# Weighting of v and the next tile's scores in one block, with the scores in the transposes' PSUM banks

## The chip, the cores and the metric

The kernel runs on one core of a Trainium2 chip. The metric is the device time of one execution in microseconds; the time given for a kernel is the median of its timed runs. Inside the core TensorE multiplies matrices into PSUM (eight banks), VectorE (DVE in the profile), ScalarE (ACT) and GpSimd (POOL) work on vectors, and the DMA queues move data between the chip's memory and the on-chip buffers. The engines run beside each other and wait for one another through semaphores.

## The reference

Attention within chunks of 64 tokens, for 8 batches, 8 heads, 576 tokens and 64 values per head. Its output, with the heads laid side by side (512 values per token), goes through a Fourier mix over tokens and values, a normalisation and a two-layer network with a hidden size of 2048:

```python
scores = scale * np.matmul(q_c, k_c.transpose(0, 1, 2, 4, 3))     # q_c, k_c, v_c: (8, 8, 9, 64, 64)
scores = scores - np.max(scores, axis=-1, keepdims=True)
attn = np.exp(scores)
attn = attn / (np.sum(attn, axis=-1, keepdims=True) + 1e-09)
x = np.matmul(attn, v_c)                                          # then laid out as (8, 576, 512)
...
X = np.fft.fft(x, axis=1)
X = np.fft.fft(X, axis=2)
u = x + np.real(X).astype(np.float32)
un = (u - mu) / np.sqrt(var + 1e-06)                              # over the 512 values
ch = np.maximum(un @ w_ch1, 0.0) @ w_ch2                          # w_ch1: 512x2048, w_ch2: 2048x512
return u + ch
```

All is in 32-bit floats; q, k, v and the weights arrive as 64-bit floats.

## The kernel before

**Tiles.** A tile is two chunks of 64 tokens with all heads: 128 rows by 512 values. A batch has nine chunks, so four tiles, and the ninth chunks of two batches make one tile more, which belongs to the even one: batches 0, 2, 4, 6 have five tiles, the odd ones four. For each tile n there are four steps of attention, called T, S, P and V here:

```python
    def att_T(n):                      # T: q and k of a tile, transposed
        if n >= first[2]:              # from the third batch on by VectorE, in stream transposes
            for src, dst, nm in ((qs, qT, "qT"), (ks, kT, "kT")):
                ...
                nc.vector.transpose(out=to.rearrange("p j c (r t) -> p j t c r", t=4), in_=a)
                if low:
                    nc.gpsimd.tensor_copy(t[:, :, :, 0:1], t[:, :, :, CH:CH + 1])
            if n + 1 < NT:
                load(n + 1)
            return
        ...                            # before that by TensorE (turn), copied out of PSUM by ScalarE

    def att_S(n):                      # S: 16 products of 64x64
        a, b = qT.pop(n), kT.pop(n)
        sc = ps_a.tile([128, 2, 512], FP32, tag="att", name="sc")
        ...
    def softmax(n):                    # maximum and difference on VectorE, exponential on ScalarE
        sc = scs.pop(n)
        ...
        nc.vector.tensor_reduce(out=mx, in_=s4, axis=AX.X, op=ALU.max)
        nc.vector.tensor_tensor(out=ex..., in0=s4, in1=mx..., op=ALU.subtract)
        nc.scalar.activation(out=ex, in_=ex, func=ACTF.Exp, scale=scale)

    def att_P(n):                      # P: the weights, transposed by TensorE, copied out by ScalarE
        ex = es.pop(n)
        pt = turn(lambda j: ex[:, j].rearrange("p e k -> p (e k)"))
        t = one_p.tile([128, NJ, 128], FP32, tag="pT", name="pT")
        nc.scalar.copy(t, pt)

    def att_V(n):                      # V: 16 products of 64x65, then sums and division on VectorE
        ...
            xp = ps_a.tile([128, 2, 512], FP32, tag="att", name="xp")
        ...
```

A 32-bit matmul is two passes of TensorE in the profile: the 16 matmuls of S or V count as x32 there.

**PSUM.** Two buffers of one bank serve all transposes (`turn`, four of 128x128 each) and the Fourier products; one buffer of two banks serves scores and weighted v in turn; four of one bank serve the network:

```python
    ps_t = ctx.enter_context(tc.tile_pool(name="ps_t", bufs=2, space=bass.MemoryType.PSUM))
    ps_a = ctx.enter_context(tc.tile_pool(name="ps_a", bufs=1, space=bass.MemoryType.PSUM))
    ps_f = ctx.enter_context(tc.tile_pool(name="ps_f", bufs=4, space=bass.MemoryType.PSUM))
```

**The side work of a batch.** The attention and the Fourier mix of batch b run in small steps (each `yield` ends one) between the steps of the network of an earlier group of four tiles:

```python
        for n in range(lo, hi + 1):
            att_S(n)
            softmax(n)
            yield
            if n + 1 < NT and (b > 0 or n < hi):
                att_T(n + 1)
            yield
            if n > lo:
                att_V(n - 1)
                ...
                yield ready(n - 1)
            att_P(n)
            yield
        att_V(hi)
```

**The network.** Nine groups of four tiles; the first groups use plain products, the later ones seven products in place of eight on halves (`up_halves` from group 2, `down_halves` from group 1). In `up_halves`, for each of four pairs r = 0, 1 of hidden blocks, products o = 0 to 6 are made, two blocks each, and read as follows (line numbers of the profile in the comments; L974 is the matmul):

```python
                    dst = (pas, pas, pbs, pbs, pas, pbs, pbs)[o][r][:, (0, 1, 0, 1, 0, 0, 1)[o]]
                    ...
                    if o == 0:
                        nc.scalar.copy(a, dst)                                            # L979
                    elif o == 1:
                        nc.vector.tensor_tensor(out=b, in0=dst, in1=a, op=ALU.add)        # L981
                    elif o == 2:
                        nc.vector.tensor_tensor(out=a, in0=dst, in1=b, op=ALU.add)        # L983
                    elif o == 3:
                        nc.vector.tensor_tensor(out=h1[:, HF + m, hi], in0=dst, in1=a, op=ALU.add)
                        ...
                if o in (1, 3, 5, 6):
                    yield h1
```

`pas[r]` and `pbs[r]` are one bank each. A step of side work follows each `yield`. `down_halves` (matmul L1021) has the same seven products and yields after each block; among them stand `normed` (the normalised tile `un` of the next group) and, one block later, `turned` (its transposes by `turn`, copied to `unT` by ScalarE or VectorE). In group 0's `down_plain` they stand so:

```python
            for j in range(G):
                due = KF - (G - j + 1)
                if m == due - 1:
                    normed(g + 1, j)
                if m == due:
                    turned(g + 1, j)
```

**The start.** Batch 0's attention (`attention_early`) and Fourier mix (`fourier_early`) run ahead of the network. The weights are made from 64-bit to 32-bit floats in 32 pieces by `round_next`: five VectorE operations and three ScalarE operations a call, each call finishing the piece of the one before. Two calls stand at the end of `attention_early`, one behind `fourier_early`, the others between the network's steps, ahead of the relus that ScalarE makes of the first products.

Of the kernel before, what the change touches and what calls it, by code (L numbers as in the profile page):

```python
# [8 lines left out]
FP32 = mybir.dt.float32  # L9
# [7 lines left out]
def kernel(  # L17
# [38 lines left out]
    NM = 2  # L56
    NT = 2 * 2 * NM + 1
# [15 lines left out]
    two_p = ctx.enter_context(tc.tile_pool(name="two", bufs=2))  # L73
    three_p = ctx.enter_context(tc.tile_pool(name="three", bufs=3))
    sm_p = ctx.enter_context(tc.tile_pool(name="sm", bufs=4))
    ps_t = ctx.enter_context(tc.tile_pool(name="ps_t", bufs=2, space=bass.MemoryType.PSUM))
    ps_a = ctx.enter_context(tc.tile_pool(name="ps_a", bufs=1, space=bass.MemoryType.PSUM))
    ps_f = ctx.enter_context(tc.tile_pool(name="ps_f", bufs=4, space=bass.MemoryType.PSUM))
    dram = ctx.enter_context(tc.tile_pool(name="dram", bufs=1, space=bass.MemoryType.DRAM))
# [35 lines left out]
    tiles, first = [], []  # L115
# [8 lines left out]
    NT = len(tiles)  # L124
# [159 lines left out]
    def round_weight(i):  # L284
# [15 lines left out]
        if 0 < i <= len(pieces):  # L300
# [8 lines left out]
                free.append(r)  # L309
            load_weight(max(raws, default=i - 1) + 1)  # L310

    def turn(src):

        pt = ps_t.tile([128, 4, 128], FP32, tag="pt", name="pt")
        for j in range(4):
            nc.tensor.transpose(pt[:, j, :], src(j), ident)  # L316
        return pt
# [39 lines left out]

    def att_S(n):
        a, b = qT.pop(n), kT.pop(n)
        sc = ps_a.tile([128, 2, 512], FP32, tag="att", name="sc")  # L360
        for j in range(NJ):
            for e in range(2):
                for c in range(2):
                    r0, t0 = e * D, c * CH
                    nc.tensor.matmul(
                        out=sc[t0:t0 + CH, e, j * CH:(j + 1) * CH],
                        lhsT=a[r0:r0 + D, 2 * j + c, 0:CH],
                        rhs=b[r0:r0 + D, 2 * j + c, 0:CH],
                        start=True,
                        stop=True,  # L370
                    )
        scs[n] = sc
# [16 lines left out]
    def att_P(n):  # L389
# [4 lines that stand above are left out]
        pT[n] = t  # L394
# [111 lines left out]
    def attention_early():  # L506

        lo, hi = first[0], first[1] - 1

        def ready(n):  # L510
            if n == at[LO, 0, 1]:
                shift_early(0)
            if n == at[HI, 0, 1]:
                fold(0, 1)
            if n == at[HI, 0, 0]:
                fold(0, 0)
            if n + 3 > hi:
                load_v(n + 3)

        att_T(lo)  # L520
        att_S(lo)
        for n in range(lo, hi + 1):
            if n < hi:
# [4 lines that stand above are left out]
                ready(n - 1)  # L528
            if n < hi:
                att_S(n + 1)  # L530
            if n in (lo, hi):
                keep_warm(1)
            att_P(n)
        shift_early(1)
        fold(0, NM)
        keep_warm(1)
        att_V(hi)
        ready(hi)
        keep_warm(3)
        turn_tables()  # L540
        round_next()
        round_next()

    def attention(b):

        lo, hi = first[b], first[b + 1] - 1

        def ready(n):

            if n == at[LO, b, NM - 1]:  # L550
                shift(b)
            for i in range(NM):
                if n == at[HI, b, i]:
                    fold(b, i)
            if n == at[HI, b, 0]:
                fold(b, NM)
            return kind(n) == HI

        if b < 2:
            att_T(lo)  # L560
            yield
        for n in range(lo, hi + 1):
            att_S(n)
            softmax(n)
            yield
            if n + 1 < NT and (b > 0 or n < hi):
                att_T(n + 1)
            yield
            if n > lo:
                att_V(n - 1)  # L570
                if n + 2 < NT:
                    load_v(n + 2)
# [4 lines that stand above are left out]
        if hi + 3 < NT:  # L577
            load_v(hi + 3)
        yield ready(hi)
# [16 lines left out]
    def fourier(b):  # L596
# [10 lines left out]
            )  # L607

        for pair in range(2):
            z = [ps_t.tile([128, 512], FP32, tag="pt", name="z") for _ in range(2)]  # L610
            for k in range(2):
                T = 2 * pair + k
                for i in range(NM):
                    product(T, i, z[k][:, 0:NQ], pm[i][:, T * HQ:(T + 1) * HQ], i == 0, False)
            for k in range(2):
                product(2 * pair + k, NM, z[k][:, 0:NQ], pm[NM][:, pair * HQ:(pair + 1) * HQ], False, True)
            mids = []
            if pair == 1:

                for g, c0 in enumerate(range(0, NQ, NS)):  # L620
                    c1 = min(c0 + NS, NQ)
                    mids.append((c0, c1, z[0][32 * g:32 * g + 1, NQ:NQ + c1 - c0]))
                for i in range(NM + 1):
                    for c0, c1, out_ in mids:
                        one = pm[i][:, DM:DM + 1] if i < NM else pm[i][:, 2 * HQ:2 * HQ + 1]
                        product(5, i, out_, one, i == 0, i == NM, slice(c0, c1))
            for k in range(2):
                T = 2 * pair + k
                nc.scalar.copy(zf[:, T, :], z[k][:, 0:NL])
                nc.scalar.copy(zr[:, h, T, 0:NQ - NL], z[k][:, NL:NQ])  # L630
                upper, mirrored = zr[:, h, T, NQ - NL:CH], z[k][:, NQ - 2:NL:-1]
                nc.scalar.activation(out=upper, in_=mirrored, func=ACTF.Copy, scale=-1.0 if pair else 1.0)
                for c0, c1, from_ in mids if k == 0 else ():
                    n = max(0, min(c1, NL) - c0)
                    if n > 0:
                        nc.scalar.copy(zf[0:1, T, c0:c0 + n], from_[:, 0:n])
                    if c1 > NL:
                        nc.scalar.copy(zr[0:1, h, T, 0:NQ - NL], from_[:, n:])
                        nc.scalar.copy(zr[0:1, h, T, NQ - NL:CH], from_[:, NQ - 2 - c0:NL - c0:-1])
            yield  # L640

        def mixed(i):
            mix = ps_t.tile([128, 512], FP32, tag="pt", name="mix")
            if i == NM:
                parts = [(j * CH, CH, zr[:, j]) for j in range(2)]
            else:
                parts = [(0, 128, zf[:, :, 128 * i:128 * (i + 1)])]
            for p0, np_, zt in parts:
                o = mix[p0:p0 + np_]
                for T, (cols, tab) in enumerate((  # L650
                    (slice(0, HM + 1, 2), ce),
                    (slice(1, HM, 2), co),
                    (slice(0, DM, 2), cx),
                    (slice(HM + 1, DM, 2), so),
                )):
                    nc.tensor.matmul(
                        out=o[:, cols], lhsT=zt[:, T], rhs=tab,
                        start=(T == 0), stop=(T == 3), skip_group_check=True,
                    )
            y = three_p.tile([128, XW], FP32, tag="y", name="y")  # L660
            nc.scalar.copy(y[:, 0:HM + 1], mix[:, 0:HM + 1])
            nc.scalar.copy(y[:, DM:DM + 1], mix[:, 0:1])
            return y, mix
# [19 lines left out]
    def fourier_early():  # L683
# [3 lines left out]
        zf = one_p.tile([128, 4 * NL + 64], FP32, tag="zf", name="zf")  # L687
        zf = zf[:, 0:4 * NL].rearrange("p (t f) -> p t f", t=4)
        pm = [pms.pop((0, i)) for i in range(NM + 1)]
        z = [ps_t.tile([128, 512], FP32, tag="pt", name="z") for _ in range(2)]  # L690
        more = ps_a.tile([128, 2, 512], FP32, tag="att", name="more_z")
        z += [more[:, k] for k in range(2)]
        mid = ps_f.tile([128, 512], FP32, tag="ff", name="mid")
# [2 lines left out]
        for i in order:  # L696
            at_ = {"start": i == order[0], "stop": i == order[-1], "skip_group_check": True}
            for T in range(4):
                p = slice(0, 128) if i < NM else slice(T % 2 * CH, T % 2 * CH + CH)
# [20 lines left out]
        for T in range(4):  # L720
# [3 lines left out]
            if T == 2:  # L724
                n = NL - c0
# [195 lines left out]
    def down_plain(g, h1):  # L921
# [4 lines left out]
        for m in range(KF):  # L926
# [15 lines left out]
                    store(n, o)  # L942
            for j in range(G):
                due = KF - (G - j + 1)
                if m == due - 1:
                    normed(g + 1, j)
                if m == due:
                    turned(g + 1, j)
                    if j >= 2 and g + 1 >= first_of[1]:
                        combined(g + 1, j - 2)  # L950
# [123 lines left out]
    with tc.manual_schedule():  # L1074
# [29 lines left out]
        def round_next():  # L1104
            nonlocal n_w
            if n_w <= len(pieces):
                round_weight(n_w)
                n_w += 1
# [4 lines left out]
        for step, _ in enumerate(fourier_early()):  # L1113
            if step == 0:
                turn_dim_tables()
        round_next()
        PAUSE = 3

        def side(b):
# [6 lines left out]
        sizes = []  # L1126
        for b in range(1, B):
            n_tiles = first[b + 1] - first[b]
            sizes.append(4 * n_tiles + PAUSE + 2 + NM + b % 2 + (b == 1))
        done, cur = 0, 0  # L1130
        begin = [0]
        for g in range(NG):
# [96 lines left out]
```

## Time and profile before

| | |
|---|---|
| time, median of 3 runs | 1124.13 us (1123.25 to 1126.62) |
| span of the profiled execution | 1122.2 us |
| VectorE busy | 571.0 us, 51% of the span |
| ScalarE busy | 298.3 us, 27% |
| scores on TensorE (L365) | 1152 passes of 64x64 |
| weighting of v on TensorE (L407) | 1152 passes of 64x65 |

In the page and in the timeline a line names engine, source line, operation, what is written and read, and the shape. A timeline line begins with the start and the length in us; a run of like instructions is one line with its count. Matmuls overlap, so lengths of neighbours add up to more than the time that passes; the starts are what to measure by. What stands in brackets is idle time of the engine before the line, and who ended it.

### The profile page before, as it was taken

The numbers are of one execution on the slowest core, as the hardware profiler recorded it, in microseconds if no ns is written. First come the engines' busy times: TensorE is split into PE (matmuls) and PEld (weight loads), VectorE is DVE, ScalarE is ACT, GpSimd is POOL, SyncE is SP. The second block draws the span as 40 slices with busy tenths as digits, with TensorE's granted clock in tenths as the row PEclk, the third lists the DMA queues.
The fourth block names the chain that finished last, engine by engine and source line by source line (L and its number), as shares of the span: only waits on it lengthen the run. The fifth ranks groups of instructions, "written<-read, shape, count | busy, mean of one in ns | idle before, by whom it ended". The sixth has DMA issues, their size and how long they took to land. (4 is left out here: it accounts for less than half of the span.)

```text
span 1122.2 us, 18759 instructions
## 1 busy us (share of the span) xinstructions
PE 1090.6 (97%) x7042; PEld 845.3 (75%) x7042; DVE 571.0 (51%) x1206; ACT 298.3 (27%) x725; POOL 276.3 (25%) x403
## 2 busy tenths in 40 slices
PE   8899999999999999999999999899999999999998
PEld 6544454446888888788888888778888888888887
DVE  4799987332555365563555355635454434323521
ACT  4688443221112311322122212221132102201210
POOL 4200003235404240063105230154024400130130
PEclk9999999999999999999999999999999999999999
DMA  8777647678475536772567356853654346446332
GB/s 171 226 195 180 158 147 236 179 233 294 149 226 163 160 137 215 213 212 79 177 194 214 114 178 199 226 157 110 194 199 113 113 144 204 141 149 195 89 113 75
DMA packets 147969, 192.72 MB, mean 172 GB/s; under 512 B 66126, under 2 KB 104014, under 8 KB 140712
## 3 DMA queue, kind: packets, MB, share of 16 engines
q1 hardware_dynamic: 145768, 190.46, 56.1%
q8 instruction: 56, 0.92, 0.3%
q0 software_dynamic: 512, 0.68, 0.3%
q10 hardware_dynamic: 1600, 0.39, 0.2%
q14 instruction: 33, 0.27, 0.1%
HBM read 167.22 MB, written 24.12 MB: 171 GB/s over the span
## 5 line engine op out<-in xcount | busy, mean ns | idle before, releaser
L880 POOL TENSOR_TENSOR h<-h 128x256 f32<-128x256 f32 x64 | 55.5, 873 | 412.7 <-PE pb L974 303.5
L1021 PE MATMUL pa<-wb,h 128*128 128x256 f32 x512 | 116.1, 381 | 0.0
L1021 PE MATMUL pb<-wb,h 128*128 128x256 f32 x512 | 115.0, 381 | 0.0
L974 PE MATMUL pb<-unT,wa 128*128 128x256 f32 x448 | 106.6, 381 | 4.1 <-DVE wa L983 4.1
L974 PE MATMUL pb<-wa 128*128 128x256 f32 x448 | 107.3, 382 | 1.1 <-DMA wa<-s 1.1
L974 PE MATMUL pa<-unT,wa 128*128 128x256 f32 x448 | 107.8, 383 | 0.0
L1021 PEld LDWEIGHTS pa<-wb,h 128*128 128x128 f32 x512 | 95.8, 190 | 14.6 <-issue 1.6
L1021 PEld LDWEIGHTS pb<-wb,h 128*128 128x128 f32 x512 | 95.8, 190 | 12.9
L974 PEld LDWEIGHTS pb<-unT,wa 128*128 128x128 f32 x448 | 84.3, 190 | 18.3 <-DVE wa L983 6.8
L974 PEld LDWEIGHTS pb<-wa 128*128 128x128 f32 x448 | 83.4, 190 | 14.3 <-DVE wa L981 1.5
L974 PEld LDWEIGHTS pa<-unT,wa 128*128 128x128 f32 x448 | 83.2, 190 | 11.6
L989 ACT ACTIVATE h<-pa 128x256 f32<-128x256 f32 x56 | 21.5, 383 | 176.1 <-PE pa L974 143.1
L890 PE MATMUL up<-unT,wa 128*128 128x512 f32 x128 | 58.0, 599 | 2.4 <-ACT h L898 1.6
L981 DVE TENSOR_TENSOR wa<-pa,wa 128x256 f32<-128x256 f32 x56 | 23.8, 425 | 70.6 <-PE pa L974 70.6
L928 PE MATMUL dn<-wb,h 128*128 128x512 f32 x128 | 57.7, 599 | 1.3 <-ACT h L898 1.3
L1021 PE MATMUL pa<-wb,yall 128*128 128x256 f32 x256 | 58.2, 382 | 0.0
L974 PE MATMUL pa<-wa 128*128 128x256 f32 x224 | 54.1, 384 | 3.8 <-ACT wa L979 3.8
L907 PE MATMUL up<-unT,wa 128*128 128x512 f32 x128 | 57.5, 598 | 0.0
L1021 PE MATMUL pb<-wb,yall 128*128 128x256 f32 x256 | 57.1, 380 | 0.0
L1021 PE MATMUL pb<-wb 128*128 128x256 f32 x256 | 56.6, 379 | 0.0
L1021 PEld LDWEIGHTS pb<-wb 128*128 128x128 f32 x256 | 48.2, 190 | 6.3
L1021 PEld LDWEIGHTS pa<-wb,yall 128*128 128x128 f32 x256 | 47.7, 190 | 6.9 <-issue 0.5
(233 smaller groups left out, 1646.0 us busy)
## 6 DMA issues: line engine op xcount, KB each, us to landing
wb<-s SPq DMA_DIRECT2D x56, 1024.0 KB
wa<-s SPq DMA_DIRECT2D x196, 256.0 KB
xall<-in_moe_w_ch_dram SPq DMA_DIRECT2D x22, 512.0 KB
q<-in_q_dram SPq DMA_DIRECT2D x96, 112.0 KB
k<-in_k_dram SPq DMA_DIRECT2D x96, 112.0 KB
v<-in_v_dram SPq DMA_DIRECT2D x124, 64.0 KB
yall<-in_moe_w_ch_dram SPq DMA_DIRECT2D x10, 512.0 KB
s<-wb SPq DMA_DIRECT2D x20, 256.0 KB
```

The costliest lines, as they stand in the source:

```text
L880: nc.gpsimd.tensor_tensor(out=h1[:, m, hi], in0=h1[:, m, lo], in1=h1[:, m, hi], op=ALU.subtract)
L890: nc.tensor.matmul(out=up, lhsT=w1[:, kk, m * 128:(m + 1) * 128], rhs=unT[:, kk], start=(kk == 0), stop=(kk == KD - 1),)
L907: nc.tensor.matmul(out=up, lhsT=w1[:, kk, m * 128:(m + 1) * 128], rhs=unT[:, kk], start=(kk == 0), stop=(kk == KD - 1),)
L928: nc.tensor.matmul(out=dn, lhsT=h1[:, m, s * 128:(s + 1) * 128], rhs=w2[:, m, :], start=(m == 0), stop=(m == KF - 1),)
L974: nc.tensor.matmul(out=dst, lhsT=w[:, kk, r], rhs=rhs[o][:, kk], start=(o in (0, 2) and kk == 0), stop=(kk == 1), skip_group_check=True,)
L981: nc.vector.tensor_tensor(out=b, in0=dst, in1=a, op=ALU.add)
L989: nc.scalar.activation(out=h1[:, m, lo], in_=dst, func=ACTF.Relu)
L1021: nc.tensor.matmul(out=dst, lhsT=lhs[:, m], rhs=w[:, m], start=(o in (0, 2) and m == 0), stop=(m == HF - 1), skip_group_check=True,)
```

## The change

From the third batch on the steps of a tile become T of the next tile, P, and then V with the next tile's S directly behind it. Both V and S use TensorE in blocks of 64x64, so that the mode of the array is switched once for both. V and S follow each other without a gap only if they have different PSUM: the scores go into the two banks of the transposes, which become one tensor with its halves handed out in turn. A batch has 3n+1 steps of attention for its n tiles in place of about 4n. Besides, one call of `round_next` moves from ahead of the early Fourier mix to behind it, and in group 0's `down_plain` the normalisation stands one step earlier.

```diff
-    ps_t = ctx.enter_context(tc.tile_pool(name="ps_t", bufs=2, space=bass.MemoryType.PSUM))
+    ps_t = ctx.enter_context(tc.tile_pool(name="ps_t", bufs=1, space=bass.MemoryType.PSUM))
...
+    two_banks = ps_t.tile([128, 2, 512], FP32, name="two_banks")
+    n_bank = 0
+
+    def bank():
+        nonlocal n_bank
+        n_bank += 1
+        return two_banks[:, n_bank % 2]
+
     def turn(src):
-        pt = ps_t.tile([128, 4, 128], FP32, tag="pt", name="pt")
+        pt = bank().rearrange("p (j t) -> p j t", j=4)
...
     def att_S(n):
         a, b = qT.pop(n), kT.pop(n)
-        sc = ps_a.tile([128, 2, 512], FP32, tag="att", name="sc")
+        sc = two_banks if n >= first[2] else ps_a.tile([128, 2, 512], FP32, tag="att", name="sc")
...
         keep_warm(3)
         turn_tables()
         round_next()
-        round_next()
...
+        if b > 1:
+            att_S(lo)
+            softmax(lo)
             yield
+            for n in range(lo, hi + 1):
+                if n + 1 < NT:
+                    att_T(n + 1)
+                yield
+                att_P(n)
+                yield
+                att_V(n)
+                if n < hi:
+                    att_S(n + 1)
+                    softmax(n + 1)
+                if n + 3 < NT:
+                    load_v(n + 3)
+                yield ready(n)
+            return
...
-                if m == due - 1:
+                if m == due - 2:
                     normed(g + 1, j)
...
         round_next()
+        round_next()
         PAUSE = 3
...
-            sizes.append(4 * n_tiles + PAUSE + 2 + NM + b % 2 + (b == 1))
+            sizes.append((4 * n_tiles + 1 if b == 1 else 3 * n_tiles + 1) + PAUSE + 2 + NM + b % 2)
```

In the cuts the Fourier products too take their banks from `bank()`.

More of the change, by code (lines that the diff above doesn't have):

```diff
@@ L557, in ready @@
             return kind(n) == HI
-        if b < 2:
-            att_T(lo)
+        if b > 1:
+            att_S(lo)
+            softmax(lo)
             yield
+            for n in range(lo, hi + 1):
[12 more added lines that the diff above has]
+            return
+        att_T(lo)
+        yield
         for n in range(lo, hi + 1):
@@ L565, in attention @@
             yield
-            if n + 1 < NT and (b > 0 or n < hi):
+            if n + 1 < NT:
                 att_T(n + 1)
@@ L609, in fourier @@
         for pair in range(2):
-            z = [ps_t.tile([128, 512], FP32, tag="pt", name="z") for _ in range(2)]
+            z = [bank() for _ in range(2)]
             for k in range(2):
@@ L642, in mixed @@
         def mixed(i):
-            mix = ps_t.tile([128, 512], FP32, tag="pt", name="mix")
+            mix = bank()
             if i == NM:
@@ L689, in fourier_early @@
         pm = [pms.pop((0, i)) for i in range(NM + 1)]
-        z = [ps_t.tile([128, 512], FP32, tag="pt", name="z") for _ in range(2)]
+        z = [bank() for _ in range(2)]
         more = ps_a.tile([128, 2, 512], FP32, tag="att", name="more_z")
```

## The prediction

> **What bounds the kernel now.** I read the page first: TensorE is busy 97% of the span and its granted clock is full in every slice, so a gain must come from TensorE's own stream, and whatever makes it wait is paid in full.
>
> ```profile
> PE 1090.6 (97%) x7042; PEld 845.3 (75%) x7042; DVE 571.0 (51%) x1206; ACT 298.3 (27%) x725; POOL 276.3 (25%) x403
> ```
>
> Next came TensorE's timeline, one line per run of like matmuls with its start. A run's real cost is the next line's start less its own. The run of eight 128x256 passes at 571.76 is followed at 573.49: 0.216 us a pass, so sixteen cost 3.45 us. Here are runs around scores (L365) and weighting of v (L407), both in 64x64 mode:
>
> ```profile
> 541.27 3.62 PE L1021 MATMUL pa<-wb,h 128*128 128x256 f32 x16
> 544.82 0.69 PE L365 MATMUL sc<-kT,qT 64*64 64x64 f32 x32
> 545.45 3.72 PE L1021 MATMUL pa<-wb,h 128*128 128x256 f32 x16
> 549.00 0.60 PE L316 MATMUL pt<-ident,un 128*128 128x128 f32 x4
> ...
> 556.35 0.60 PE L316 MATMUL pt<-ident,un 128*128 128x128 f32 x4
> 556.88 0.70 PE L407 MATMUL xp<-v,pT 64*64 64x65 f32 x32
> 557.51 3.72 PE L1021 MATMUL pb<-wb,h 128*128 128x256 f32 x16
> ```
>
> Both runs of sixteen take 3.55 us: 0.10 lost entering the 64x64 block and 0.10 leaving it. The block is 0.63, so each S or V costs 0.83 us.
>
> Third, TensorE's waits (who waited for whom, us in all, times, longest), of which these matter:
>
> ```profile
> PE pb L974 <- DVE wa L983: 4.1, 4, 1.0
> PE pa L974 <- ACT wa L979: 3.8, 7, 0.5
> PE pt L316 <- ACT un L783: 1.7, 1, 1.7
> ...
> PE up L890 <- ACT h L898: 1.6, 1, 1.6
> ```
>
> The timeline of all engines shows where the second comes from:
>
> ```profile
> 565.05 0.70 PE L365 MATMUL sc<-kT,qT 64*64 64x64 f32 x32
> ...
> 565.67 1.99 PE L974 MATMUL pa<-unT,wa 128*128 128x256 f32 x8
> 565.81 0.69 DVE L378 TENSOR_REDUCE mx<-sc 128x8 f32<-128x512 f32 x1 [0.16 <-PE sc L365]
> 566.54 0.69 DVE L380 TENSOR_TENSOR ex<-sc,mx 128x512 f32<-128x512 f32 x1
> 567.26 0.63 ACT L386 ACTIVATE ex<-ex 128x512 f32<-128x512 f32 x1 [4.92 <-DVE ex L380]
> ...
> 567.80 0.63 ACT L979 COPY wa<-pa 128x256 f32<-128x256 f32 x2
> ...
> 568.21 1.99 PE L974 MATMUL pa<-wa 128*128 128x256 f32 x8 [0.54 <-ACT wa L979]
> ```
>
> Product 1 of an up stage may not write until product 0's copy (L979) has left the same bank. The copy stands behind the exponential (L386) in ScalarE's queue, and that behind the softmax on VectorE. Product 1 starts 2.54 us after product 0; 1.83 would do. So S ahead of product 0 costs 0.7 us.
>
> **What the Trainium skill says.** "TensorEngine Tiling (Array Packing)", section Tiling Modes, says that changing the tiling mode drains TensorE; the 0.10 in and 0.10 out agree. "PSUM — Partial Sum Buffer", section PSUM bank collisions raise a hardware error, asks for guarding PSUM by bank and quadrant, not by address; the wait on L979, for the other half of one bank, agrees. Its section Engine vs sequencer instructions calls ScalarE's and VectorE's queues strict FIFO; L979 running right behind L386 agrees.
>
> **The change part by part.** Positions are from the order of instructions in the two built programs.
>
> *Merges.* Batches 2 to 7 have 5, 4, 5, 4, 5, 4 tiles, and V(n) with S(n+1) meet in all but a batch's last tile: 4+3+4+3+4+3 = 21. Two blocks cost 2 x 0.83 = 1.66 now. Merged, the first costs only its issue: 32 weight loads of 134 ns take 0.56 us, so (0.56 - 0.134)/31 = 14 ns apart, 0.44 in all; then 0.63 and 0.20 for one switch pair, 1.27. That saves 0.39; I take 0.35 for a seam between them. 21 x 0.35 = **-7.4 us**.
>
> *S shares the transposes' banks.* In batches 3 to 7 the first S directly follows the transposes of un, as before, but must now wait for their copy:
>
> ```profile
> 532.21 0.63 PE L316 MATMUL pt<-ident,un 128*128 128x128 f32 x4 [0.32 <-DVE un L785]
> ...
> 532.76 0.69 PE L365 MATMUL sc<-kT,qT 64*64 64x64 f32 x32
> 532.87 0.58 ACT L798 COPY unT<-pt 128x512 f32<-128x512 f32 x1 [1.01 <-PE pt L316]
> ```
>
> The copy ends at 533.45, so S moves from 532.76 to about 533.5: 5 x 0.75 = **+3.8**. In each of six batches the order un, V, S occurs once too: S could start 1.0 after un's start, the copy is out at 1.3: 6 x 0.3 = **+1.8**.
>
> *V and S load VectorE together.* V's normalisation now stands ahead of the softmax. From the timeline of a V without S behind it: V at T (577.04), its first VectorE step at T+0.81 (577.85), the last one gives way at T+1.86 (578.90); then L378, L380, L386 and L979 follow 0.73, 0.72, 0.54 apart, and product 1 0.41 later: T+4.26. TensorE alone would be there at T + 0.44 + 0.63 + 0.10 + 1.73 = T+2.90, so the wait is 1.36 us in place of 0.70. Odd batches (3, 5, 7) have one pair ahead of product 0: 3 x 0.66 = **+2.0**. Even ones (4, 6) have two, and a third one product earlier that I put at 0.8, against two waits of 0.7 before: 2 x (2 x 1.36 + 0.8 - 1.4) = **+4.2**.
>
> *The L983 wait.* Product 3 waits until product 2's sum (L983) has left its bank. In odd batches a pair now stands right after product 1; the softmax ends at T+3.3, the sum at T+3.7, TensorE is there at T+2.9: 0.8 against 0.1 now, 3 x 0.7 = **+2.2**. In even batches the two stream transposes (L333, 2.06 us) that cause 1.1 us of this wait stand before L983 three times, not twice: 2 x 1.1 = **+2.2**.
>
> *Start.* One rounding moves behind the early transform. Now it ends at 40.06 and holds up VectorE's first copy; without it the copies' chain ends some 1.0 us earlier. But from 50.98 to 69.23 VectorE runs seven roundings without a gap (18.25/7 = 2.61 each), and the first relu (68.98), for which TensorE waits, is queued behind the last. Eight roundings from 49.94 end at 70.8: **+1.6**.
>
> *Group 1's transposes.* Normalising one step earlier removes the 1.7 us wait on L783. But the first of these transposes now needs the softmax of the S one step ahead to have left its bank, and VectorE is full there (3.68 of 171 to 175 us): S's L380, with two more differences for the weights ahead of it, ends near 177.8 and TensorE arrives at 176.75. The wait falls from 1.7 to 1.1: **-0.6**.
>
> *Transforms.* In odd batches the two halves stand one product closer: some 0.15 each, **+0.4**.
>
> Sum: -7.4 + 3.8 + 1.8 + 2.0 + 4.2 + 2.2 + 2.2 + 1.6 - 0.6 + 0.4 = +10.2 us, 1134 us. Several of these waits assume that the engine behind is as late as in one traced case, and waits following each other partly hide; I take 2 to 3 us off: **1131.5 us**.
>
> **Rivals.** (1) *Merges alone count.* The new waits are mostly hidden, and -7.4 with the start near zero gives 1116 to 1119. For it: TensorE is the bound and a switch is measured. Against: products 1 and 3 already wait on exactly these copies, with 0.5 and 1.0 us at a time, and the change puts more ahead of them. (2) *Shared banks dominate.* Should a copy or softmax be late by a whole product, transposes and S would wait 2 us each, some 10 of them: 1140 to 1145. Against: ScalarE is 27% busy, and three to seven us lie between S and the next transposes. (3) *Input loads.* q and k have one buffer each; a later transpose delays the next load. VectorE waits only 3.1 us on q in all, so I expect under 1 us.
>
> **Range and chances.** The sum's largest errors are the saving per merge (0.23 to 0.45 makes 4.8 to 9.5 us) and the 8.4 us for the merged pairs' waits (2.0 + 4.2 + 2.2), which could halve or grow by half. Range 1120 to 1139. The sum with all its errors stays far inside 2% (22 us): faster by over 2% 0.01, within 0.97, slower by over 2% 0.02.
>
> **What would show it.** Right: L407 followed by L365 within 0.5 us; TensorE's wait on L979's successor up from 3.8 us to 9 or more; a new wait of S on ScalarE's copy of unT, about 0.7 each, five times; TensorE resuming after the first relu near 71.2, not 69.6. Wrong: those waits absent and 1118 or less, or L365 starting a full 0.7 us after L407 (no merge gain).

## The result, and the profile after

The changed kernel takes **1168.98 us**, the median of six runs (1164.69 to 1169.95), against 1123.87 for the kernel before on the same chip: a ratio of 1.0395, 95% interval 1.0375 to 1.0415. The prediction was 1131.5 with a range up to 1139, so it is 37 us short. The profiled execution, the fastest of the six, spans 1162.9 us, 40.7 more than before.

The page of the changed kernel, its line of busy times: TensorE works on the same 7042 matmuls for 4.6 us longer, and the rest of the loss is idle time.

```profile
PE 1095.2 (94%) x7042; PEld 851.9 (73%) x7042; DVE 575.8 (50%) x1206; ACT 298.8 (26%) x725; POOL 277.6 (24%) x403
```

Next its list of TensorE's waits (who waits for whom, us in all, times, longest). Line numbers have moved by 9 to 27: L1001 is the up stage's matmul (L974 before), L1006 and L1010 the copy and the sum that were L979 and L983, L325 the transposes (L316), L374 S, L416 V.

```profile
PE two_banks L325 <- ACT qT L353: 11.3, 9, 2.4
PE pb L1001 <- DVE h L1018: 10.2, 3, 5.7
PE pa L1001 <- ACT wa L1006: 9.0, 9, 1.2
PE pb L1001 <- DVE wa L1010: 7.8, 9, 1.0
PE two_banks L325 <- DVE unT L823: 3.5, 4, 0.9
PE two_banks L374 <- ACT unT L825: 3.4, 5, 0.7
PE two_banks L325 <- ACT pT L402: 2.1, 3, 0.7
PE up L917 <- DVE wa L306: 2.0, 1, 2.0
```

Of these eight, three were predicted: L1006 (3.8 before), L1010 (4.1 before) and S on the copy of unT. The rounding L306 comes from the step that was moved, but the prediction had it hold up the first relu, and here it holds up the first product as well. The first, second, fifth and seventh were not predicted, and they are the larger part: 27.1 us.

The first of the unpredicted ones, in the timeline of the changed kernel, TensorE and ScalarE, during batch 1 (start, duration, operation; in brackets the idle time before it and its releaser):

```profile
80.58 0.60 PE L325 MATMUL two_banks<-ident,q 128*128 128x128 f32 x4
...
82.02 0.72 ACT L299 ACTIVATE power<-power,top 128x512 uint32<-128x512 uint32 x1
82.64 0.57 ACT L353 COPY qT<-two_banks 128x512 f32<-128x512 f32 x1
83.27 0.66 PE L325 MATMUL two_banks<-ident,k 128*128 128x128 f32 x4 [2.09 <-ACT qT L353]
```

q's transposes go to one half of two_banks, k's to the other. Yet k's wait 2.09 us for the copy that empties q's half, and that copy stands behind a weight's rounding on ScalarE (L299 is its last step). In the kernel before, the same two groups ran back to back:

```profile
85.59 0.60 PE L316 MATMUL pt<-ident,q 128*128 128x128 f32 x4
86.03 0.60 PE L316 MATMUL pt<-ident,k 128*128 128x128 f32 x4
```

The second, in batch 3. SyncE's DMA queue of the changed kernel first (start, time of issuing, transfer, how many):

```profile
348.71 1.21 SPq L469 DMA_DIRECT2D first<-xall  x2
...
354.14 1.10 SPq L472 DMA_DIRECT2D xall<-first  x2
...
358.26 6.01 SPq L192 DMA_DIRECT2D q<-in_q_dram  x8
364.37 3.66 SPq L192 DMA_DIRECT2D k<-in_k_dram  x8
```

then VectorE:

```profile
369.81 1.08 DVE L342 STREAM_TRANSPOSE kT<-k 128x512 f32<-128x512 f32 x1 [2.73 <-DMA k<-in_k_dram]
370.74 0.73 DVE L1018 TENSOR_TENSOR h<-pb,wa 128x256 f32<-128x256 f32 x2
```

and TensorE:

```profile
363.65 1.89 PE L1001 MATMUL pb<-unT,wa 128*128 128x256 f32 x8
371.19 3.78 PE L1001 MATMUL pb<-wa 128*128 128x256 f32 x8 [5.65 <-DVE h L1018]
```

The exchange of border rows (shift) writes out rows at 348.7, waits for them to land, and writes back at 354.1. The next tile is the first of an even batch; its 16 small loads of q and k stand behind that. VectorE's transpose T of that tile waits for k until 369.81 and holds up the sum L1018 behind it in VectorE's queue, and product 6 of the up stage waits for that sum: 5.65 us, after which its eight matmuls need 3.78 us in place of 1.89. Batch 5 shows the same, with a wait of 4.14 us. In the kernel before, these loads were issued ahead of the shift:

```profile
333.27 7.16 SPq L192 DMA_DIRECT2D q<-in_q_dram  x8
340.53 5.34 SPq L192 DMA_DIRECT2D k<-in_k_dram  x8
...
349.75 1.22 SPq L460 DMA_DIRECT2D first<-xall  x2
```

The chain that was predicted is there almost to the hundredth. The changed kernel's timeline of TensorE around V, S and products 0 and 1:

```profile
593.44 0.70 PE L416 MATMUL xp<-v,pT 64*64 64x65 f32 x32
593.95 0.65 PE L374 MATMUL two_banks<-kT,qT 64*64 64x64 f32 x32
594.53 2.00 PE L1001 MATMUL pa<-unT,wa 128*128 128x256 f32 x8
597.68 1.99 PE L1001 MATMUL pa<-wa 128*128 128x256 f32 x8 [1.16 <-ACT wa L1006]
```

V to S takes 0.51 us and S to product 0 0.58: one switch pair instead of two. Product 1 starts 4.24 us after V (predicted: 4.26).

### The profile page after: what moved, and what is told of

It is laid out like the page before. It is cut to its first block, busy times and chain, and to the rows that moved or that the text cites. A ratio compares the mean times of both kernels' runs of the same rounds, so it can differ in the third digit from the quotient of the medians.

```text
span 1162.9 us, 18725 instructions
## 1 busy us (share of the span) xinstructions
PE 1095.2 (94%) x7042; PEld 851.9 (73%) x7042; DVE 575.8 (50%) x1206; ACT 298.8 (26%) x725; POOL 277.6 (24%) x403
## 5 line engine op out<-in xcount | busy, mean ns | idle before, releaser
L1001 PE MATMUL pb<-wa 128*128 128x256 f32 x448 | 110.7, 392 | 10.2 <-DVE h L1018 10.2
L1001 PE MATMUL pb<-unT,wa 128*128 128x256 f32 x448 | 106.8, 382 | 7.8 <-DVE wa L1010 7.8
L1001 PE MATMUL pa<-unT,wa 128*128 128x256 f32 x448 | 107.2, 383 | 0.0
L1001 PEld LDWEIGHTS pb<-wa 128*128 128x128 f32 x448 | 85.2, 194 | 24.7 <-DVE h L1018 11.7
L1001 PEld LDWEIGHTS pb<-unT,wa 128*128 128x128 f32 x448 | 84.3, 190 | 22.6 <-DVE wa L1010 11.4
L1001 PEld LDWEIGHTS pa<-unT,wa 128*128 128x128 f32 x448 | 84.7, 192 | 11.2
L1001 PE MATMUL pa<-wa 128*128 128x256 f32 x224 | 53.9, 384 | 9.0 <-ACT wa L1006 9.0
L934 PE MATMUL up<-unT,wa 128*128 128x512 f32 x128 | 56.8, 596 | 0.0
L1001 PEld LDWEIGHTS pa<-wa 128*128 128x128 f32 x224 | 40.9, 190 | 18.8 <-ACT wa L1006 12.8
L402 ACT COPY pT<-two_banks 128x512 f32<-128x512 f32 x36 | 20.9, 581 | 127.9 <-PE two_banks L325 127.9
```

The source lines that it names most:

```text
L934: nc.tensor.matmul(out=up, lhsT=w1[:, kk, m * 128:(m + 1) * 128], rhs=unT[:, kk], start=(kk == 0), stop=(kk == KD - 1),)
L1001: nc.tensor.matmul(out=dst, lhsT=w[:, kk, r], rhs=rhs[o][:, kk], start=(o in (0, 2) and kk == 0), stop=(kk == 1), skip_group_check=True,)
```

## The experiments

Theory A: the two banks are now one tensor, and every use of one half waits until the other half has been emptied. Theory B: the next batch's loads stand behind the shift in SyncE's queue. Rival to both: the new order of V and S as such.

**e1_one_tensor.** The kernel before, with only its buffers for transposes and transforms replaced; scores stay in ps_a, and no instruction moves.

```diff
+    two_banks = ps_t.tile([128, 2, 512], FP32, name="two_banks")
+    def bank(): ...; return two_banks[:, n_bank % 2]
-        pt = ps_t.tile([128, 4, 128], FP32, tag="pt", name="pt")
+        pt = bank().rearrange("p (j t) -> p j t", j=4)
     # z and mix likewise; ps_t has bufs=1
```

> The kernel before with one thing of the change: its two one-bank buffers for transposes and transforms become one two-bank tensor whose halves are used in turn. Scores stay in their own banks, and no instruction moves. Theory A (halves of one tensor are guarded as a whole, so each use waits for the copy that empties the other half): k's transposes wait for ScalarE's copy of q's in each of the ten tiles that are turned on TensorE, 1 to 1.5 us a tile, +13 to +17 us (about 1137 to 1141). Rival (the new order of V and S made the start late): nothing of that order is here, so within 2 us of 1124.

Measured: 1148.17 us beside 1124.23 for the kernel before, ratio 1.0215 (1.0199 to 1.0230): 24 us from this edit alone. TensorE's waits of e1:

```profile
PE two_banks L324 <- ACT qT L352: 11.4, 9, 2.4
PE two_banks L324 <- DVE unT L804: 6.3, 7, 0.9
PE pb L982 <- DVE wa L991: 4.1, 4, 1.0
PE pa L982 <- ACT wa L987: 3.7, 7, 0.5
```

The waits of k's transposes are those of the changed kernel (11.4 and 11.3), and the copy and the sum (L987, L991) wait as in the kernel before. A holds. I had expected at most 17, having counted only q and k; P's transposes behind those of un wait as well (6.3, seven times), and 5.1 us more are lost to a slower clock behind three of the waits on qT (last section).

**e2_two_tensors.** The changed kernel with the banks as two tensors.

```diff
-    two_banks = ps_t.tile([128, 2, 512], FP32, name="two_banks")
+    banks = [ps_t.tile([128, 512], FP32, name=f"bank{i}") for i in range(2)]
-        return two_banks[:, n_bank % 2]
+        return banks[n_bank % 2]
-                        out=sc[t0:t0 + CH, e, j * CH:(j + 1) * CH],
+                        out=sc[e][t0:t0 + CH, j * CH:(j + 1) * CH],    # softmax: maximum and difference per half
```

> The changed kernel, with the two banks as two tensors: transposes take them in turn, scores write one half in each, and the softmax's maximum and difference run once per half. Theory A: the waits of k's transposes on ScalarE's copy of q's go, and so do those of P's transposes on the copy of un's: 15 to 19 us less than the changed kernel, 1150 to 1154. Rival (order alone): 1166 to 1171, with VectorE's two shorter steps in place of one long one adding at most 2.

Measured: 1148.00 us, 1.0203 (1.0181 to 1.0226), 21 less than the changed kernel. No wait of L325 on qT is left in its list. A again, by some 2 us more than expected.

**e3_shift_later.** The changed kernel with the shift one T later, and so behind the loads that this T issues.

```diff
-            if n == at[LO, b, NM - 1]:
+            if n == at[LO, b, NM - 1] and b < 2:
                 shift(b)
...
                 if n + 1 < NT:
                     att_T(n + 1)
+                if n == at[HI, b, 0]:
+                    shift(b)
                 yield
```

Only batches from the third on go through this loop.

> The changed kernel, with the transfers that exchange border rows (shift) issued behind the next tile's VectorE transposes and so behind that tile's successor's q and k loads, as in the kernel before; banks as changed. Theory B (the 16 small loads of the next batch's first tile stood in SyncE's queue behind the shift's round trip): the waits of TensorE on L1018's relu by way of kT and qT in batches 3 and 5 go, 13 to 16 us less than the changed kernel, 1153 to 1156. Rival (VectorE is too full for these transposes anyway): at most 3 us less.

Measured: 1157.15 us, 1.0290 (1.0275 to 1.0305), 11.8 less than the changed kernel. From its waits:

```profile
PE pa L1003 <- DMA wa<-s: 2.5, 2, 1.5
...
PE pb L1003 <- DVE h L1020: 1.0, 3, 0.4
```

The wait on the sum falls from 10.2 to 1.0 us. B holds. The gain is short of 13; the slabs of weights (wa) now come late twice, 2.5 us, which may be the reason but was not tested.

**e4_both.** The changed kernel with both edits, the diffs of e2 and e3.

> The changed kernel with both: two tensors for the two banks and the shift behind the next loads. If A and B are separate causes their savings add: 28 to 35 us less than the changed kernel, 1134 to 1141, which leaves +10 to +17 over the kernel before for the terms that the prediction had (+10.2 by its sum). If they overlap (one stall hides the other), 1145 or more.

Measured: 1137.48 us, 1.0122 (1.0107 to 1.0137), 31.5 less than the changed kernel, where the two alone give 21.0 and 11.8: they nearly add. 13 us over the kernel before are left. Its waits:

```profile
PE pa L1018 <- ACT wa L1023: 11.3, 9, 1.4
PE pb L1018 <- DVE wa L1027: 8.6, 9, 1.0
PE bank L379 <- ACT unT L842: 2.9, 5, 0.7
PE up L934 <- DVE wa L306: 2.0, 1, 2.0
```

These are the prediction's own terms and the rounding. The copy's wait is 2.3 us longer than in the changed kernel; the softmax runs in four shorter steps here, which is the likely reason, though no run changes that alone.

The next four take those terms on one at a time, each on top of the one before, the first on top of e4.

**e5_v_in_banks.** As e4, but V in the two banks and S in ps_a, with a whole softmax. The diff is against the changed kernel and leaves out e3's.

```diff
-        sc = two_banks if n >= first[2] else ps_a.tile([128, 2, 512], FP32, tag="att", name="sc")
+        sc = ps_a.tile([128, 2, 512], FP32, tag="att", name="sc")
+        elif n >= first[2]:
+            xp = banks, None          # in att_V; its division in two halves, as in batch 0
```

> The kernel of e4_both with the two places exchanged: the weighting of v writes into the transposes' two banks (as two tensors, its division in two halves), and scores have the other two banks for themselves, with a softmax in whole steps. Theory (the wait of S on the copy of un comes from S being in the transposes' banks; V needs P's copy anyway, so there it waits for nothing new): the 2.9 us of S on unT go, the rest stays, 1133 to 1136. Rival (un's next transposes now wait for V's division instead): 1137 to 1140.

Measured: 1136.01 us (1132.51 to 1139.36), 1.0108 (1.0082 to 1.0134): not told apart from e4. The theory fell. S no longer waits for un's copy, but V does, as its waits show, for V follows un's transposes in the same step six times:

```profile
PE bank L418 <- ACT unT L829: 3.3, 6, 0.7
```

**e6_scores_first.** S ahead of V in the merged block.

```diff
-                att_V(n)
                 if n < hi:
                     att_S(n + 1)
                     softmax(n + 1)
+                att_V(n)
```

> e5_v_in_banks with S(n+1) ahead of V(n) in each merged block, so that the softmax stands ahead of the division on VectorE. Theory (the extra wait of product 1 on product 0's copy, 1.41 or 1.16 us, is the softmax standing behind the division): that wait falls to 0.3 to 0.6, nine times, 5 to 8 us less than e5, 1127 to 1130; the merge keeps its one switch pair. Rival (VectorE's sum of both is what counts, not their order): the wait moves to products 2 and 3, and less than 2 us is gained.

Measured: 1126.75 us, 1.0017 (1.0005 to 1.0029), 9.3 less than e5. Of its waits:

```profile
PE pb L1005 <- DVE wa L1014: 8.1, 9, 1.0
...
PE pa L1005 <- ACT wa L1010: 0.7, 2, 0.4
```

The wait on the copy falls from 10.3 to 0.7, further than expected, and the sum's stays at 8.1: for the copy, the order on VectorE is what cost, not the sum of both. V's wait of 3.3 us for un's copy is gone from the list too, as S now stands between them, so the 9.3 us are not the softmax's place alone.

**e7_transposes_split.** T of q and T of k in two steps; the shift moves with T of k.

```diff
                 if n + 1 < NT:
-                    att_T(n + 1)
+                    att_T(n + 1, (0,))       # q
                 yield
+                if n + 1 < NT:
+                    att_T(n + 1, (1,))       # k, and load(n + 2)
                 att_P(n)
```

> e6_scores_first with the VectorE transposes T of q and of k in two steps, 1.03 us each, the second ahead of P. Theory (product 3 waits 1.04 us for product 2's sum because 2.06 us of T stand ahead of it, in even batches three times): these waits on the sum nearly go, 4 to 7 us less than e6, 1121 to 1126. Rival (the second half only moves the wait, to products 5 and 6 or to P's copy): within 2 us of e6.

Measured: 1125.63 us, 1.0013 (1.0000 to 1.0027), about 1 less than e6, from which the intervals do not tell it apart. The theory's 4 to 7 us did not come, and the rival had the size. The waits on the sum fell from nine to five but not in total, for one is now 3.9:

```profile
PE pb L1007 <- DVE wa L1016: 8.0, 5, 3.9
```

**e8_round_back.** e7 with the moved rounding step back at the start.

```diff
         turn_tables()
         round_next()
+        round_next()          # and one fewer behind the early transform
```

> e7_transposes_split with the one rounding step back ahead of the early transform, as in the kernel before. Theory (the prediction's start term: VectorE's stretch of seven roundings became eight and holds the first relu): 1 to 2 us less than e7, with group 0's down stage starting that much earlier. Rival (the early transform starts that much later instead): within 0.5 us of e7.

Measured: 1123.02 us, 0.9988 (0.9976 to 1.0000), 2.6 less than e7; the wait of "up" on the rounding (L306, 2.0) is gone. The long wait of e7 is still there, and e8's timeline of VectorE and TensorE shows it:

```profile
465.99 1.08 DVE L342 STREAM_TRANSPOSE qT<-q 128x512 f32<-128x512 f32 x1 [3.28 <-DMA q<-in_q_dram]
```

```profile
462.01 1.89 PE L1008 MATMUL pb<-wa 128*128 128x256 f32 x8
467.38 3.40 PE L1008 MATMUL pb<-unT,wa 128*128 128x256 f32 x8 [3.48 <-DVE wa L1017]
```

T of q is one step ahead of T of k now, but its load was still issued only behind T of the previous tile's k, and so came too late: theory B's kind of stall, made by my own edit. The rival of e7 named another place for it.

**e9_loads_by_part.** e8 with each load behind its own T.

```diff
-            if n + 1 < NT and 1 in part:
-                load(n + 1)
+            if n + 1 < NT:
+                load(n + 1, part)     # q behind T of q, k behind T of k
```

> e8_round_back with the next tile's q loaded right behind T of q and its k right behind T of k, so that q's loads are queued one step earlier. Theory (what ate the gain of the split is one wait of T on a late q load in batch 4, 3.5 us plus 1.5 of a slower run behind it): it goes, 3 to 6 us less than e8, 1117 to 1120, under the kernel before by 0.3 to 0.6%. Rival (the load is late because the transfers as a whole are, whatever the order of issue): within 1.5 us of e8.

Measured: **1117.73 us** (1114.57 to 1119.80), 0.9945 (0.9927 to 0.9963), 5.3 less than e8 (4.8 by the two ratios, as e8 ran on another chip) and the best of all: it beats the kernel before by 0.4 to 0.7%. TensorE's timeline and waits of e9:

```profile
562.96 1.99 PE L1009 MATMUL pa<-unT,wa 128*128 128x256 f32 x8
565.02 1.99 PE L1009 MATMUL pa<-wa 128*128 128x256 f32 x8
```

```profile
PE pb L1009 <- DVE wa L1018: 1.9, 3, 0.6
```

Product 1 follows product 0 after 2.06 us, where the changed kernel needs 3.15 and the kernel before 2.54, and the sum's waits are 1.9 in all.

**e10_unmerged.** e9 with S and V in separate steps of the stream. A batch again has 4n steps in place of 3n+1.

```diff
                     att_S(n + 1)
                     softmax(n + 1)
+                    yield
                 att_V(n)
```

> e9_loads_by_part with a step of the stream between S(n+1) and V(n), so that each of the 21 pairs becomes two blocks with their own switches; all else as e9. Theory (a merge saves 0.35 us, as the prediction had it, and with the softmax first it costs little elsewhere): 5 to 9 us more than e9. Rival (the crowding of VectorE by S and V together eats the saving): within 2 us of e9, or less than it.

Measured: 1123.62 us, 1.0000 (0.9990 to 1.0010), 5.9 more than e9. So a merge is worth 5.9/21 = 0.28 us, 0.2 to 0.4 by the two intervals. That is the price of the whole step and not of the switch alone, for with 4n steps all later steps fall on other products too. In its list of waits the copy is back at 3.8 us (0.7 in e9) and seven times, as in the kernel before:

```profile
PE pa L1010 <- ACT wa L1015: 3.8, 7, 0.5
```

## Why the prediction was wrong

**The step that failed first: "S shares the transposes' banks".** It looked only at what S, the new user, would wait for. The same edit had turned the two buffers into two halves of one tensor for all the old users too: q's and k's transposes, P's, un's and the transforms. The page "PSUM — Partial Sum Buffer" of the Trainium skill, section PSUM bank collisions raise a hardware error, which the prediction cites, asks for a guard by bank and quadrant; the two halves are different banks, so that rule needs no wait here. The runs show a wait that goes with the tensor: in e1 it comes with it, in e2 it leaves with it, while the banks stay the same two. It costs 21 us of the changed kernel (e2), 24 in the old order (e1). Most of it falls in the first two stages, where ScalarE also rounds weights and a copy is late by 2 us; the down stage of group 0 starts 17.1 us later in e1 than in the kernel before, and 15.7 in the changed kernel. (The prediction read the old L979 wait as one by bank; that pair too is two halves of one tensor, and no run here tells the two readings apart.)

**The second: rival 3, "I expect under 1 us".** The sum of VectorE's waits on q, 3.1 us, said what the loads cost where they stood. It said nothing of where they would stand. The loads of the next tile are issued by T; the change left T's place nearly alone but moved V, and with it the shift, ahead of them in SyncE's queue. This cost 11.8 us (e3) or 10.5 (e2 to e4).

**Rival 2, "Shared banks dominate", came nearest.** Its 16 to 21 us are the size of the first cause (21 in e2), not of the whole loss, and late copies with waits of 2 us are part of what happened. Both arguments that put it aside failed. Three to seven us between S and the next transposes holds and is beside the point, for the transposes wait for each other. ScalarE's 27% is a mean over the kernel: from 50 to 110 us, where it also rounds weights, it is busy 50.1 of 60 us in the kernel before.

**What was right.** The four signs that the prediction named for being right came, or nearly: V to S in 0.51 us for 0.5, a wait on the copy of 9.0 us, S on unT five times, and TensorE resuming after the first relu at 70.91 (e4) for 71.2. The time missed all the same, since each sign tested a term on the list. Nearly all of these terms can be read off, and they fit. *Merges*: 0.35 a pair predicted; the trace has 0.51 + 0.58 = 1.09 us from V to product 0 and 0.20 for the one switch pair, 1.29 against two blocks of 0.83, so 0.37, and e10 measures 0.28 net. *S on un's copy*: +3.8 predicted, 3.4 measured, five times; with V between them S starts 0.83 us after V in place of 0.51, six times, so the 0.3 each that were predicted. *V and S load VectorE together*: 2.0 + 4.2 predicted, 9.0 - 3.8 = 5.2 measured. *The L983 wait*: 4.4 predicted (3 x 0.7 is 2.1, not 2.2), 7.8 - 4.1 = 3.7 measured. *Start*: +1.6 predicted; in e4, whose first product starts when that of the kernel before does (52.53 and 52.51), the first relu comes at 70.28 against 68.98, +1.3; e8, which puts the rounding back, gains 2.6. *Group 1's transposes*: -0.6 predicted; group 0's plain down stage, in which they stand, takes 74.09 us in e4 and 74.84 before, -0.75. *Transforms*, +0.4, is too small to be told in any run. Their sum of +10.2 meets e4, where both causes are taken away: +13.2, of which 2.3 are likely to come from the softmax in halves. Taking 2 to 3 us off for terms hiding each other was not borne out.

**The range** was formed from the errors of the terms on the list. Its fault was that it held nothing for a term not on the list, though the diff touches three helpers that the argument never followed. Its chance for slower by over 2% was 0.02.

**What stays open.** Profiles whose code is the same up to there show the first product of group 0 between 52.5 us (e4) and 56.8 (e5). Of these 4.3 us, 1.35 are there when the early transform starts, after a longer wait (e4, then e5), and the rest is a slower clock behind that wait, at which the first four matmuls take 2.26 us in place of 1.21:

```profile
31.35 1.21 PE L745 MATMUL bank<-tk,pm 128*128 128x289 f32 x4 [1.81 <-POOL pm_rest L525]
```

```profile
32.70 2.26 PE L732 MATMUL bank<-tk,pm 128*128 128x289 f32 x4 [2.96 <-POOL pm_rest L512]
```

Why that wait differs is not known. Of the 5.6 us that the changed kernel's first product is later, 5.5 are there when the fourth V of batch 0 starts (30.14 us against 24.62), among the waits of its transposes on qT and pT (0.67 to 0.74 us each); e1 is 6.1 late at that place.

## What to carry to other kernels

When buffers are pooled into one tensor, ask for every old user, not only the new one, which wait the sharing adds; two tensors of one bank each keep the banks independent at the same cost in space. When a step moves, follow the transfers it issues through their in-order queue: a short exchange with a round trip in it holds up all loads that now stand behind it. And in a merged block, put first the half whose result starts the longer chain on another engine: scores before the weighting of v was worth 9 us, more than the merging itself.

## What the runs showed of the hardware that I had not expected

A wait of TensorE can be paid twice. The stretches of the changed kernel around the 5.65 us wait (window, its length, busy us of TensorE, weight loads, VectorE, ScalarE and GpSimd, then the granted clock, the DMA share and GB/s):

```profile
365.00:371.00 6.00, 0.54 (x3) 0.14 (x1) 2.80 (x4) 0.00 (x0) 3.62 (x8) 0.91 0.65 173
371.00:375.00 4.00, 3.81 (x10) 2.99 (x11) 0.89 (x3) 1.37 (x3) 0.00 (x0) 0.50 1.02 263
375.00:380.00 5.00, 5.00 (x36) 4.18 (x38) 0.96 (x3) 1.85 (x4) 0.00 (x0) 0.83 1.05 255
```

The clock is 0.50 for the first 4 us of work after it and back at full by 380; the run of eight took 3.78 us for 1.89. In e8, 3.48 us of waiting were followed by a run of 3.40. Worked out from the two slow stretches above, 4.00 x 0.50 + 5.00 x 0.17 = 2.9 us of TensorE's time were lost on top of the wait itself, an estimate.

Shorter waits can do it too. In e1 the three waits on qT of batch 1 (2.09, 2.44 and 2.44 us) are each followed by eight matmuls that take 5.30 us in place of 3.60, as here:

```profile
97.82 0.66 PE L324 MATMUL two_banks<-ident,k 128*128 128x128 f32 x4 [2.44 <-ACT qT L352]
98.31 5.30 PE L898 MATMUL up<-unT,wa 128*128 128x512 f32 x8
```

The clock is 0.63 from 98 to 102 us there. Three times 1.7 makes 5.1 of e1's 24 us. In the changed kernel only one of these three waits had a slow run behind it (4.65 us). The Trainium skill, "TensorE: Matmul & The Clock Gate", section Part 1: The HAM clock gate, puts the fall to half rate at about 3.4 us without work. The waits of 5.65 and 3.48 us are past that; those of 2.09 and 2.44 us are not, unless the transposes around them count for nothing, so the length of one wait does not settle it here. The mean granted clock of the profiled executions is 0.992 in the changed kernel and 0.999 before, which makes 0.008 x 1162.9 = 9.3 us against 1.1. By this estimate up to 8 of the 40.7 us are the slower clock; the part that falls in waits costs nothing.
